# Batches of 768 tokens, 384 columns a matmul, in the last three products of an attention and two-MoE kernel

## The chip, the cores and the metric

The kernel runs on one core of one Trainium2 chip. The metric is the device time of one execution in microseconds. A core has a matrix engine (TensorE; PE in the profile, its weight loads PEld), a vector engine (DVE), a scalar engine (ACT), GpSimd (POOL) and SyncE (SP), which here issues all transfers, one after the other, from a single queue.

## What is computed

```python
# q, k, v: (8, 8, 576, 64), phi: (8, 8, 576, 32)
a = softmax(phi, axis=2)
k_m = einsum('bhsm,bhsd->bhmd', a, k)
v_m = einsum('bhsm,bhsd->bhmd', a, v)
attn = softmax(q @ k_m.T / 8) @ v_m
x = attn as 4608 tokens x 512
x = relu(x @ moe_w_in) ** 2 @ moe_w_out
h = x @ moe2_w_in
out = (h * sigmoid(h)) @ moe2_w_out        # 512 -> 2048 -> 512, twice
```

All is float32, and the weights come as float64 words, which the kernel itself turns into float32.

## The kernel before

Every product works on float32 numbers that are split into a high and a low part, and takes three matmuls for one (high by high, high by low, low by high). Four stages follow each other.

- **Stage 0** is the attention and the first MoE product (`front`, `first_product`, matmuls at L464), for eight batches of 576 tokens. Its result goes to DRAM in quarters, `g1`, one DMA for two of the sixteen rows of features (L476).
- **Stage 1** is the second MoE product, by `second` (matmuls at L641). **Stage 2** is the third product, by the loop at L718 (matmuls at L731). **Stage 3** is the fourth, by `second` again. These are the last three products of the title.

Stages 1 to 3 use Winograd's form of Strassen's scheme: a product of two-by-two blocks in seven block products instead of eight. `PRODUCTS` (L522) gives their seven right-hand sides in order, n = 0 to 6: B11, B21, T2, T1, T3, B22, T4. The T are differences of quarters of the tokens' matrix, and the seven left-hand sides are combinations of the weights, which `combine` makes on ACT and DVE in the stage before, writes to DRAM (L179) and `load_w` (L519) brings back. A tile `W[q]` holds all seven combinations for 256 rows or columns of the weights, q = 0 to 7; all eight tiles stay in SBUF for a stage. A combination with its high and low part is 256 KB.

A stage takes the tokens in eight batches of 576, as two halves of 288 columns. In `second` a batch is 7 products of 4 steps (h) of 12 matmuls, 336 in all, and the first and last product are 28 steps apart. Three steps ahead (`AHEAD`), `combos` makes the operand of a step: ACT casts the high part (L612), DVE subtracts it for the low part (L613); for n = 2 DVE makes four differences before (L602 T1, L604 T3, L608 T2, L609 T4). The quarters of a batch lie in six places that rotate from batch to batch (`places`, `NAMES`, `FREED`). In stage 2 a batch is four rounds r of two q, and a round is 7 products of 12 matmuls. `evict` adds and copies the sums out of PSUM.

A scheduler decides each engine's order; the instructions of an engine and the transfers of SP's queue then run strictly in that order, and a transfer that waits holds back those behind it. `hold` ties the background work of `combine` to a step of the product.

Of the kernel before, what the change touches and what calls it, by code (L numbers as in the profile page):

```python
# [18 lines left out]
P = 128  # L19
# [11 lines left out]
W4 = 512  # L31

# [3 lines left out]
GT = 3  # L36
# [29 lines left out]
def attention_moe_moe(ctx: ExitStack, tc, q, kv, phi, w_in1, w_out1, w_in2, w_out2, out):  # L66
# [53 lines left out]
    NQ = NF // 2  # L120
# [32 lines left out]
    def combine(key, srcs, following=None, whole=None, parts=None, step=None):  # L153
# [15 lines left out]
        def split(to, of):  # L169

            if whole is not None:
                hi, lo = whole[:, to, 0], whole[:, to, 1]
            else:
                part = prep.tile([P, 2, 2 * P], F32, tag="pp", bufs=2, name="pp")
                hi, lo = part[:, 0].bitcast(F32R), part[:, 1]
            held(nc.scalar.copy(hi, w[:, of]))  # L176
            tt(lo, w[:, of], hi.bitcast(F32), op=ALU.subtract)  # L177
            if whole is None:
                nc.sync.dma_start(parts[:, to], part)  # L179
# [48 lines left out]
    def load_unit(j, i):  # L228

        n = 2 * j + i  # L230
        if n < 3 * (NQ // 2):
            if n % 3 == 0:
                staged["w"] = wr.tile([P, 7, 4 * P], F32, tag=f"w{n // 3}", name="st")
            st = staged["w"].rearrange("p i c -> p (i c)")[:, n % 3 * 4 * PC:(n % 3 + 1) * 4 * PC]
        else:
            if i == 0:
                staged[j] = work.tile([P, 2, 2, W4], F32, tag="ring", bufs=RING, name="st")
# [13 lines left out]
    def front(b):  # L251
# [23 lines left out]
        def load_q(r):  # L275
            if b == 0 and r == 2:
                t = work.tile([P, 2, 2, HALF], F32, tag="gt", bufs=GT, name="q")
                t = t.rearrange("p a b n -> p (a b n)")[:, :NP * RT].rearrange("p (k n) -> p k n", k=NP)
# [170 lines left out]
    def quarters_tiles(n):  # L449
        return [dram.tile([P, NQ, 4, HALF], F32, tag=f"{n}_{b}", name=f"{n}_{b}") for b in range(B)]  # L450

# [3 lines left out]
    def first_product(t):  # L455
# [14 lines left out]
        if f % 2 == 0:  # L470
            gts[b] = work.tile([P, 2, 2, HALF], F32, tag="gt", bufs=GT, name="gt")
        gt = gts[b]
        nc.scalar.activation(gt[:, f % 2], h[:, :, :HALF], AF.Relu)  # L473
# [12 lines left out]
    for t in sorted(sched):  # L486
# [4 lines left out]
    W.update({q: wr.tile(WSHAPE, F32R, tag=f"w{q}", name=f"ws{q}") for q in range(NQ // 2)})  # L491
    background = combine_all([
        (("w1o", q), src_out(w_out1, q), {"whole": W[q]} if q in W else {"parts": w1o[q]}) for q in reversed(range(NQ))
# [22 lines left out]
    W.update({q: wl.tile(WSHAPE, F32R, tag=f"w{q}", name=f"ws{q}") for q in range(NQ // 2, NQ)})  # L516

    def load_w(src, q, n0, n1):
        nc.sync.dma_start(W[q][:, n0:n1].bitcast(F32), src[q][:, n0:n1])  # L519
# [3 lines left out]
    FIRST = (0, 1, 3)  # L523

# [27 lines left out]
    NAMES = ("B11", "B21", "B12", "B22", "T2", "")  # L552
    FREED = ("", "T2", "B11", "B12", "B22", "B21")

    def second(src, order, first_places, square, to, begin):
# [5 lines left out]
        places = [dict(zip(first_places, range(6)))]  # L561
        for _ in range(1, B):
# [3 lines left out]
        def place_tiles(b, name):  # L566

            i = places[b][name]
            if i < 2:
                t = xpool.tile([P, NQ, HALF], F32, tag="xt"[i], name="r")  # L570
                ts = [t[:, :HQ], t[:, HQ:]]
            else:
                ts = [xpool.tile([P, HQ, HALF], F32, tag="xc", bufs=8, name="r") for _ in range(2)]
# [5 lines left out]
        def quarters(b, names=("B11", "B21", "B12", "B22")):  # L579
            for name in names:  # L580
                for i, t in enumerate(place_tiles(b, name)):
                    for h in range(i * HQ, i * HQ + HQ, QS):
                        dma = nc.sync.dma_start(t[:, h - i * HQ:h - i * HQ + QS], src[b][:, h:h + QS, order.index(name)])
# [7 lines left out]
        def combos(b, n, h):  # L591
# [19 lines left out]
            c = cc[b, n, h] = spool.tile([P, 2, QS, HALF], F32R, tag="g", bufs=5, name="c")  # L611
# [3 lines left out]
        steps = [(b, n, h) for b in range(B) for n in range(7) for h in range(NH)]  # L615
# [12 lines left out]
        for k, (b, n, h) in enumerate(steps):  # L628
# [5 lines left out]
            if h == 0 and n in FIRST:  # L634
                for o in range(2):
                    ps[o][bank] = psum.tile([P, HALF], F32, tag=bank, bufs=4 if bank == "a" else 2, name=f"ps{bank}")
            x = cc.pop((b, n, h))
            for u in range(QS):
                for o in range(2):
                    for m, (wi, xi) in enumerate(((0, 0), (0, 1), (1, 0))):  # L640
                        mm = nc.tensor.matmul(  # L641
                            ps[o][bank], W[h * QS + u][:, n, wi, o * P:(o + 1) * P], x[:, xi, u],
# [3 lines left out]
                        if u == o == m == 0:  # L646
                            begun.append(mm)
            if h < NH - 1:
                continue
            for o in range(2):  # L650
                def tile_s(u, o=o):
                    if u not in st[o]:
                        st[o][u] = spool.tile([P, HALF], F32, tag=u, name=u)
                    return st[o][u]

                def done(c, bank, o=o, b=b):
                    if bank is None:
# [6 lines left out]
                evict(n, ps[o], tile_s, lambda c: tile_s(SUM[c]), nc.scalar.copy, done)  # L664

# [3 lines left out]
    x2 = [dram.tile([P, 2, NP, HALF], F32, tag=f"x2_{b}", name=f"x2_{b}") for b in range(B)]  # L669

    def begin_out1(quarters):
        quarters(0, ("B11",))
        for n, name in enumerate(("B21", "B12", "B22", None)):
            for q in range(NQ // 2, NQ):
                load_w(w1o, q, n, n + 1 if name else 7)
            if name:
                quarters(0, (name,))

    second(g1, ("B11", "B12", "B21", "B22"), ("B21", "", "B11", "B12", "B22", "T2"), True,
           lambda b, o, half: x2[b][:, half, o], begin_out1)  # L680
# [10 lines left out]
    xc = {}  # L691

    def load_x2(b):
        x = xpool.tile([P, 2, NP, HALF], F32, tag="x", name="x2")
        for half in range(2):
            nc.sync.dma_start(x[:, half], x2[b][:, half])
        tt = nc.vector.tensor_tensor
        t = xpool.tile([P, 4, 2, HALF], F32, tag="t", name="t2")
        tt(t[:, 0:2].rearrange("p h k n -> p h (k n)"), x[:, 1].rearrange("p (h k) n -> p h (k n)", h=2),
           x[:, :, 0:2].rearrange("p h k n -> p h (k n)"), op=ALU.subtract)  # L700
        tt(t[:, 2], x[:, 1, 2:4], t[:, 0], op=ALU.subtract)
        tt(t[:, 3], x[:, 0, 2:4], t[:, 2], op=ALU.subtract)
        xt[b] = {"B11": x[:, 0, 0:2], "B21": x[:, 0, 2:4], "B22": x[:, 1, 2:4],
                 "T1": t[:, 0], "T3": t[:, 1], "T2": t[:, 2], "T4": t[:, 3]}

    def split_x2(b, n):
        src = xt[b][PRODUCTS[n][0]]
        c = xc[b, n] = xpool.tile([P, 2, 2, HALF], F32R, tag="xc", bufs=8, name="xc")
        nc.scalar.copy(c[:, 0], src)
        nc.vector.tensor_tensor(c[:, 1], src, c[:, 0].bitcast(F32), op=ALU.subtract)  # L710

    load_x2(0)
    for n in range(7):
        for q in range(NQ):
            load_w(w2i, q, n, n + 1)
    for n in range(7):
        split_x2(0, n)
    for b in range(B):  # L718
        for r in range(NQ // 2):
# [3 lines left out]
            gq = {q: spool.tile([P, 4, HALF], F32, tag="g", bufs=5, name="g2t") for q in qs}  # L723
            for n, (_, bank) in enumerate(PRODUCTS):
                for q in qs:
                    if n in FIRST:
                        ps[q][bank] = psum.tile([P, HALF], F32, tag=bank, bufs=4 if bank == "a" else 2, name=f"ps{bank}")
                    x = xc[b, n]
                    for k in range(2):
                        for m, (wi, xi) in enumerate(((0, 0), (0, 1), (1, 0))):  # L730
                            mm = nc.tensor.matmul(  # L731
                                ps[q][bank], W[q][:, n, wi, k * P:(k + 1) * P], x[:, xi, k],
# [16 lines left out]
                if r == NQ // 2 - 1 and b + 1 < B:  # L749
                    split_x2(b + 1, n)  # L750
            for q in qs:
                nc.sync.dma_start(g2[b][:, q], gq[q])
            if r == 0 and b + 1 < B:
# [9 lines left out]
    def begin_out2(quarters):  # L763
        quarters(0, ("B11", "B21"))
        for q0, n0, n1 in ((0, 0, 4), (2, 0, 4), (4, 0, 2), (6, 0, 1), (6, 1, 2), (4, 2, 4), (6, 2, 3)):
            for n in range(n0, n1):
                for q in (q0, q0 + 1):
                    load_w(w2o, q, n, n + 1)
            if q0 == 6 and n0 == 1:
                quarters(0, ("B12", "B22"))  # L770
        for n in range(3, 7):
            for q in (range(NQ) if n > 3 else (6, 7)):
                load_w(w2o, q, n, n + 1)
# [48 lines left out]
```

## Time and profile before

| | us |
|---|---|
| median of 3 runs | 1471.46 (1466.14 to 1471.5) |
| the profiled execution, its time | 1474.32 |
| its span, first to last instruction | 1472.5 |
| TensorE busy | 1408.9 (96%) |
| DVE busy | 1070.2 (73%) |
| ACT busy | 825.8 (56%) |
| DMA | 321.40 MB, 218 GB/s over the span |

The time of an execution is the span and some 2 us around it. Busy times of TensorE count a matmul from its start to a modelled end, so consecutive ones overlap; its pace is read from the distance of starts.

### The profile page before, as it was taken

To read this page: it belongs to the slowest core of one execution; us is meant where nothing else is said; L and a number is where in the kernel's file an instruction comes from. 1 tells how busy PE (TensorE), PEld (TensorE's weight loads), DVE (VectorE), ACT (ScalarE), POOL (GpSimd) and SP (SyncE) were. 2 spreads that over 40 slices of the span, in tenths; PEclk is the share of its full clock that TensorE was granted. 3 is DMA by queue.
4 is the path that set the end of the run, shared out by engine and by line. 5 is a ranking of instruction groups with operands and counts; after the bars stand their busy time and mean duration, and the time that the engine had idled before them with its cause. 6 is when DMAs were issued, how large, how long until landed. Compare 5 with 4: busy or idle time off the path is not lost.

```text
span 1472.5 us, 29779 instructions
## 1 busy us (share of the span) xinstructions
PE 1408.9 (96%) x11264; PEld 1332.2 (90%) x11264; DVE 1070.2 (73%) x2078; ACT 825.8 (56%) x1582; POOL 44.6 (3%) x85
## 2 busy tenths in 40 slices
PE   4799999999999999999989999999998999999999
PEld 2567777778999999999989999999998999999999
DVE  5768787772798888998957666677536776677874
ACT  3455565566677777677545555555534444444443
POOL 2220100000000000000000000000000000000000
PEclk9899999999999999999999999999999999999999
DMA  9568988757955765458985564565599435354320
GB/s 358 164 220 306 322 318 303 242 190 269 358 176 196 238 211 193 159 196 268 328 288 200 207 229 181 208 225 220 211 397 320 121 102 157 121 153 138 112 90 33
DMA packets 184271, 321.40 MB, mean 218 GB/s; under 512 B 16192, under 2 KB 100672, under 8 KB 183616
## 3 DMA queue, kind: packets, MB, share of 16 engines
q1 hardware_dynamic: 184128, 319.50, 62.8%
q8 instruction: 88, 1.44, 0.4%
q14 instruction: 55, 0.45, 0.1%
HBM read 188.37 MB, written 131.07 MB: 217 GB/s over the span
## 4 chain that ended last, share of the span: by engine, by line
PE 66%; DVE 14%; DMA 12%; ACT 4%; issue 3%; SPq 1%; POOL 1%; ACTq 0%; POOLq 0%; DVEq 0%
PE psa L641 19%; PE psa L731 13%; PE psc L641 10%; PE h L464 7%; PE psc L731 6%; PE psb L641 4%; DVE c L613 4%; PE psb L731 3%; DMA kv<-kv 2%; DMA r<-g 2%; PE pswp L360 1%; ACT c L612 1%; DVE r L608 1%; DMA a<-phi 1%; DMA st<-moe_w_out 1%
## 5 line engine op out<-in xcount | busy, mean ns | idle before, releaser
L613 DVE TENSOR_TENSOR c<-r,c 128x576 fp32r<-128x576 f32 x448 | 332.0, 753 | 154.0 <-ACT c L612 151.3
L641 PE MATMUL psa<-c,ws 128*128 128x288 f32 x3072 | 429.3, 297 | 9.8 <-DVE c L613 6.0
L612 ACT CAST c<-r 128x576 fp32r<-128x576 f32 x448 | 298.0, 673 | 235.9 <-PE psa L641 119.9
L641 PEld LDWEIGHTS psa<-c,ws 128*128 128x128 f32 x3072 | 416.9, 190 | 13.4 <-DVE c L613 8.5
L464 PEld LDWEIGHTS h<-at,wp 128*128 128x128 f32 x1536 | 213.9, 194 | 56.7 <-ACT gt L473 26.3
L464 PE MATMUL h<-at,wp 128*128 128x288 f32 x1536 | 237.3, 308 | 14.6 <-ACT gt L473 10.4
L731 PE MATMUL psa<-xc,ws 128*128 128x288 f32 x1536 | 230.9, 296 | 4.7 <-ACT u L530 3.8
L731 PEld LDWEIGHTS psa<-xc,ws 128*128 128x128 f32 x1536 | 213.4, 188 | 5.3 <-ACT u L530 4.0
L641 PE MATMUL psc<-c,ws 128*128 128x288 f32 x1536 | 211.0, 295 | 0.0
L641 PEld LDWEIGHTS psc<-c,ws 128*128 128x128 f32 x1536 | 206.4, 188 | 0.0
L731 PE MATMUL psc<-xc,ws 128*128 128x288 f32 x768 | 118.1, 295 | 0.0
L473 ACT ACTIVATE gt<-h 128x576 f32<-128x576 f32 x128 | 82.1, 648 | 55.9 <-PE h L464 51.2
L641 PE MATMUL psb<-c,ws 128*128 128x288 f32 x768 | 109.4, 296 | 0.7 <-DVE c L613 0.7
L731 PEld LDWEIGHTS psc<-xc,ws 128*128 128x128 f32 x768 | 107.6, 188 | 0.0
L641 PEld LDWEIGHTS psb<-c,ws 128*128 128x128 f32 x768 | 104.4, 188 | 1.4 <-DVE c L613 1.4
L589 ACT ACTIVATE r<-r 128x576 f32<-128x576 f32 x128 | 85.1, 683 | 20.5 <-DMA r<-g 17.9
L176 ACT CAST pp<-pw 128x256 fp32r<-128x256 f32 x140 | 55.4, 404 | 51.0 <-DMA w1o<-pp 11.6
L177 DVE TENSOR_TENSOR pp<-pw,pp 128x256 f32<-128x256 f32 x140 | 57.4, 418 | 28.1 <-ACT pp L176 26.9
L745 ACT ACTIVATE g2t<-g2t 128x864 f32<-128x864 f32 x64 | 58.3, 923 | 31.1 <-DVE g2t L528 31.0
L530 ACT COPY u<-psa 128x288 f32<-128x288 f32 x96 | 37.5, 396 | 58.6 <-PE psa L731 40.3
L731 PE MATMUL psb<-xc,ws 128*128 128x288 f32 x384 | 63.5, 299 | 0.0
L535 ACT COPY u<-psa 128x288 f32<-128x288 f32 x96 | 37.8, 398 | 39.9 <-PE psa L731 33.4
(86 smaller groups left out, 1266.0 us busy)
## 6 DMA issues: line engine op xcount, KB each, us to landing
r<-g SPq DMA_DIRECT2D x256, 288.0 KB, 4.4
g<-gt SPq DMA_DIRECT2D x64, 576.0 KB, 4.7
g<-g2t SPq DMA_DIRECT2D x64, 576.0 KB, 4.0
kv<-kv SPq DMA_DIRECT2D x32, 516.0 KB, 6.6
st<-moe_w_out SPq DMA_DIRECT2D x64, 256.0 KB, 3.7
w2i<-pp SPq DMA_DIRECT2D x56, 256.0 KB, 3.2
ws<-w2i SPq DMA_DIRECT2D x56, 256.0 KB, 4.3
w2o<-pp SPq DMA_DIRECT2D x56, 256.0 KB, 2.7
```

The lines of the kernel that those rows point to most:

```text
L176: held(nc.scalar.copy(hi, w[:, of]))
L177: tt(lo, w[:, of], hi.bitcast(F32), op=ALU.subtract)
L464: mm = nc.tensor.matmul(h[:, half, :HALF], wp[b, j][:, g, s, fo:fo + P], attnT[b][:, x, g, tk], start=(k == 0), stop=(k == len(ops) - 1),)
L473: nc.scalar.activation(gt[:, f % 2], h[:, :, :HALF], AF.Relu)
L530: nc.scalar.copy(s("u1"), t["a"])
L535: nc.scalar.copy(s("u2"), t["a"])
L589: nc.scalar.activation(raw[b, name, h], raw[b, name, h], AF.Square)
L612: nc.scalar.copy(c[:, 0], r(name))
L613: tt(c[:, 1], r(name), c[:, 0].bitcast(F32), op=ALU.subtract)
L641: mm = nc.tensor.matmul(ps[o][bank], W[h * QS + u][:, n, wi, o * P:(o + 1) * P], x[:, xi, u], start=(n in FIRST and h == u == m == 0), sto ...
L731: mm = nc.tensor.matmul(ps[q][bank], W[q][:, n, wi, k * P:(k + 1) * P], x[:, xi, k], start=(n in FIRST and k == 0 and m == 0), stop=(k == ...
L745: nc.scalar.activation(gq[q][:, :3], gq[q][:, :3], AF.Silu)
```

## The change

- Stages 1 to 3 take six batches of 768 tokens (`TB`, `TH`): a half is 384 columns, so a matmul has 384 in place of 288, and there are three quarters as many of all instructions of a batch.
- `W[q]` holds six combinations in place of seven (`SLOTS`). Those for n = 1 and n = 6 share a place (`slot`): after product 1, `next_w` loads combination 6 over it, after product 6 combination 1 again, in every batch.
- Of the first four `W[q]`, which stage 0 fills directly, combinations 1 and 6 now go through DRAM too (`keep`).
- `second` has five places for quarters in place of six. T3 is written in the code at n = 3 and T4 at n = 4, no more at n = 2.
- Stage 0 still makes batches of 576. Its quarters go to DRAM in batches of 768, so each store is cut in two (of 384 and 192 columns). `g1` and `g2` keep a quarter's rows together.
- Sums `u1` and `u3` share buffers, `gt` has four in place of three, and the background work is held to other steps (`BEGIN2`, `PARTS`).

```diff
+TB, TH = 6, 384
-GT = 3
+GT = 4
+WR = 4
+SLOTS = 6
-STEPS = B * 7 * 4
-BEGIN2, SPREAD2 = 9, 28
-BEGIN3, SPREAD3 = 4, 24
-PARTS = (0, 1, 3, 4, 6, 8, 10, 12, 13, 15, 17, 19, 21)
+STEPS = TB * 7 * 4
+BEGIN2, SPREAD2 = 2, 20
+BEGIN3, SPREAD3 = 2, 18
+PARTS = (0, 1, 2, 3, 5, 6, 8, 9, 10, 12, 13, 15, 16)
...
-            if whole is not None:
+            keep = whole is not None and to not in (1, 6)
+            if keep:
...
-            nc.sync.dma_start(g1[b][:, u:u + 2, 2 * fh:2 * fh + 2], gt)
+            i = 0
+            while i < S:
+                to, k = divmod(b * S + i, TH)
+                n = min(TH - k, S - i)
+                nc.sync.dma_start(g1[to // 2][:, 2 * fh + to % 2, u:u + 2, k:k + n], gt[:, :, i:i + n])
+                i += n
...
+    def slot(n):
+        return n if n < SLOTS else 1
+
+    def load_w(src, q, n):
+        nc.sync.dma_start(W[q][:, slot(n)].bitcast(F32), src[q][:, n])
+
+    def next_w(src, qs, n, last):
+
+        if n == 1 or n == 6 and not last:
+            for q in qs:
+                load_w(src, q, 7 - n)
...
+    UTAG = {"u1": "u1", "u2": "u2", "u3": "u1"}
...
-    NAMES = ("B11", "B21", "B12", "B22", "T2", "")
-    FREED = ("", "T2", "B11", "B12", "B22", "B21")
+    NAMES = ("B11", "B21", "B12", "B22", "T2")
+    FREED = ("B11", "T2", "B12", "B22", "B21")
...
                 tt(r("B11"), r("B12"), r("B11"), op=ALU.subtract)
                 raw[b, "T1", h] = r("B11")
-                tt(r("B12"), r("B22"), r("B12"), op=ALU.subtract)
-                raw[b, "T3", h] = r("B12")
                 if h == 0:
                     place_tiles(b, "T2")
                 tt(r("T2"), r("B22"), r("T1"), op=ALU.subtract)
+            elif name == "T1":
+                tt(r("B12"), r("B22"), r("B12"), op=ALU.subtract)
+                raw[b, "T3", h] = r("B12")
+            elif name == "T3":
                 tt(r("B21"), r("B21"), r("T2"), op=ALU.subtract)
                 raw[b, "T4", h] = r("B21")
...
+            next_w(weights, range(h * QS, h * QS + QS), n, b == TB - 1)
...
+                next_w(w2i, qs, n, b == TB - 1)
```

Where the scheduler puts these things is seen at three places. The first is DVE at the start of stage 3, from the last but one operand of product 1 on. Before:

```order
L613 TENSOR_TENSOR c<-r,c 128x576 x3
L602 TENSOR_TENSOR r<-r 128x576
L604 TENSOR_TENSOR r<-r 128x576
L608 TENSOR_TENSOR r<-r 128x576
L604 TENSOR_TENSOR r<-r 128x576
L608 TENSOR_TENSOR r<-r 128x576
L609 TENSOR_TENSOR r<-r 128x576
L604 TENSOR_TENSOR r<-r 128x576
L608 TENSOR_TENSOR r<-r 128x576
L528 TENSOR_TENSOR u_13662<-psb,u_13662 128x288
L528 TENSOR_TENSOR u_13664<-psb,u_13664 128x288
```

Now (L620 is T1, L624 T2, L626 T3, L629 T4, L633 the low part):

```order
L620 TENSOR_TENSOR r<-r 128x768 x2
L633 TENSOR_TENSOR c<-r,c 128x768
L624 TENSOR_TENSOR r<-r 128x768
L626 TENSOR_TENSOR r<-r 128x768
L624 TENSOR_TENSOR r<-r 128x768
L626 TENSOR_TENSOR r<-r 128x768
L629 TENSOR_TENSOR r<-r 128x768
L633 TENSOR_TENSOR c<-r,c 128x768
L629 TENSOR_TENSOR r<-r 128x768
L624 TENSOR_TENSOR r<-r 128x768
L626 TENSOR_TENSOR r<-r 128x768
```

T3 and T4 still stand among the T2, ahead of product 3's operands; between the last operand of product 1 and the first of product 2 there are five differences now, where there were eight differences and two sums of `evict`.

The second place is SP's queue in the middle of stage 3, within one batch: `r<-g` loads quarters of the next batch, `out` stores results. Before:

```order
L663 DMA out<-u_14159 128x288
L663 DMA out<-u_14161 128x288
L583 DMA r<-g_2_9051 128x2x288 x9
L663 DMA out<-u_14373 128x288
L663 DMA out<-u_14375 128x288
L663 DMA out<-u_14307 128x288
L663 DMA out<-u_14309 128x288
L663 DMA out<-y 128x288 x2
```

Now (`ws` are places of the weights, loaded from `w2o`; L531 is `load_w`), from the quarters to the last result of the batch; eight more loads of the same kind, of combination 6, follow in the next batch:

```order
L602 DMA r<-g_1_8210 128x768 x11
L684 DMA out<-u_12143 128x384
L684 DMA out<-u_12145 128x384
L602 DMA r<-g_1_8210 128x768
L684 DMA out<-u_12073 128x384
L684 DMA out<-u_12075 128x384
L531 DMA ws_388<-w2o_11315 128x512
L531 DMA ws_389<-w2o_11316 128x512
L531 DMA ws_390<-w2o_11317 128x512
L531 DMA ws_391<-w2o_11318 128x512
L531 DMA ws_4535<-w2o_11319 128x512
L531 DMA ws_4536<-w2o_11320 128x512
```

Loads of weights, of which there were none inside a batch, now stand between the results of two products, in the order in which the products end.

The third place is SP's queue in the middle of stage 2, a little over one round: `g` are results, `st` and `w2o` belong to the background work. Before:

```order
L179 DMA w2o_13053<-pp 128x512 x3
L752 DMA g_4_9053<-g2t 128x1152 x2
L179 DMA w2o_13053<-pp 128x512
L752 DMA g_4_9053<-g2t 128x1152 x2
L129 DMA st<-moe_w_out 128x512
L179 DMA w2o_13054<-pp 128x512
```

Now:

```order
L531 DMA ws_4535<-w2i_7749 128x512
L531 DMA ws_4536<-w2i_7750 128x512
L183 DMA w2o_11320<-pp 128x512 x2
L132 DMA st<-moe_w_out 128x512 x2
L531 DMA ws_4535<-w2i_7749 128x512
L183 DMA w2o_11320<-pp 128x512
L531 DMA ws_4536<-w2i_7750 128x512
L779 DMA g_3_8212<-g2t 512x1x384
L531 DMA ws_4537<-w2i_7751 128x512
L779 DMA g_3_8212<-g2t 512x1x384
```

Each tile of weights is loaded twice a round (combination 6, then 1), and stores of the background work, which wait for DVE, stand between the two.

## Rows read from the trace of the kernel before

**Rows 1.** The page: engines' busy us, share of the span, instructions.
```profile
PE 1408.9 (96%) x11264; PEld 1332.2 (90%) x11264; DVE 1070.2 (73%) x2078; ACT 825.8 (56%) x1582; POOL 44.6 (3%) x85
```
**Rows 2.** Windows by stage: us, PE PEld DVE ACT POOL, clock, DMA, GB/s.
```profile
0.00:372.00 372.00, 325.60 (x3200) 253.92 (x3200) 253.03 (x574) 207.44 (x407) 44.58 (x85) 0.98 0.77 268
372.00:735.00 363.00, 360.36 (x2682) 358.19 (x2683) 324.60 (x591) 257.01 (x489) 0.00 (x0) 1.00 0.69 232
735.00:1101.00 366.00, 361.33 (x2698) 360.56 (x2697) 226.69 (x515) 187.95 (x398) 0.00 (x0) 1.00 0.64 236
1101.00:1472.50 371.50, 361.58 (x2688) 359.54 (x2686) 265.90 (x400) 173.43 (x290) 0.00 (x0) 0.99 0.43 137
```
**Rows 3.** The chain that ended last, in time: start us, us, what.
```profile
793.07 3.21 PE psa L731 x24
...
1150.36 12.75 PE psa L641 x96
1163.11 3.45 PE psb L641 x26
...
1207.74 3.45 PE psb L641 x26
```
**Rows 4.** Stage 3 near 1122 us: PE's timeline, forms, windows (as rows 2).
```profile
1122.78 5.00 PE L641 MATMUL psa<-c,ws 128*128 128x288 f32 x20
...
L641 PE MATMUL psa<-c,ws 128*128 128x288 f32 x20 | 5.0, 442 | 0.0
...
1121.10:1127.90 6.80, 5.53 (x23) 5.53 (x24) 6.57 (x11) 1.28 (x2) 0.00 (x0) 0.50 0.89 307
```
**Rows 5.** Timeline of PE around two short groups in stage 0: start us, us.
```profile
130.00 0.59 PE L310 MATMUL psmx<-dm,ones 128*128 128x256 f32 x2
130.22 0.38 PE L310 MATMUL psmx<-dm,ones 128*128 128x256 f32 x1
...
142.23 0.43 PE L464 MATMUL h<-at,wp 128*128 128x288 f32 x2
142.49 0.27 PE L347 MATMUL pst<-ident,y 128*128 128x128 f32 x1
```
**Rows 6.** Groups by form: matmuls and weight loads (busy us, mean ns of one).
```profile
L641 PE MATMUL psa<-c,ws 128*128 128x288 f32 x3072 | 429.3, 297 | 9.8 <-DVE c L613 6.0 <-ACT c L612 3.6
L641 PEld LDWEIGHTS psa<-c,ws 128*128 128x128 f32 x3072 | 416.9, 190 | 13.4 <-DVE c L613 8.5 <-ACT c L612 4.5 <-DMA ws<-w1o 0.2
L347 PEld LDWEIGHTS pst<-ident,y 128*128 128x128 f32 x32 | 4.2, 148 | 2.2 <-ACT y L338 1.6 <-issue 0.4 <-DVE wp L403 0.2
```
**Rows 7.** Groups by form: operations of DVE by length.
```profile
L613 DVE TENSOR_TENSOR c<-r,c 128x576 fp32r<-128x576 f32 x448 | 332.0, 753 | 154.0 <-ACT c L612 151.3
...
L699 DVE TENSOR_TENSOR t<-x 128x1152 f32<-128x1152 f32 x8 | 10.8, 1356 | 2.4 <-DMA x<-x 2.4
```
**Rows 8.** DMA issues: count, KB each, median us from issue to landing.
```profile
g<-gt SPq DMA_DIRECT2D x64, 576.0 KB, 4.7
...
ws<-w2i SPq DMA_DIRECT2D x56, 256.0 KB, 4.3
...
ws<-w2o SPq DMA_DIRECT2D x56, 256.0 KB, 6.0
```
**Rows 9.** Timeline of PE at the start of stage 3.
```profile
1118.68 0.42 PE L641 MATMUL psa<-c,ws 128*128 128x288 f32 x2
1122.37 8.87 PE L641 MATMUL psa<-c,ws 128*128 128x288 f32 x46 [3.27 <-DVE c L613]
```
**Rows 10.** Stage 2: SP's waits (us in total, times, longest), then SP's timeline.
```profile
SPq L179 <- DVE pp L177: 97.5, 40, 8.1
...
1089.80 9.62 SPq L519 DMA_DIRECT2D ws<-w2o  x13
```
**Rows 11.** Stage 2's start: timeline of PE.
```profile
742.27 1.81 PE L731 MATMUL psc<-xc,ws 128*128 128x288 f32 x12
747.90 2.47 PE L731 MATMUL psa<-xc,ws 128*128 128x288 f32 x12 [3.82 <-ACT u L530]
```

More of the change, by code (lines that the diff above doesn't have):

```diff
@@ L449, in quarters_tiles @@
     def quarters_tiles(n):
-        return [dram.tile([P, NQ, 4, HALF], F32, tag=f"{n}_{b}", name=f"{n}_{b}") for b in range(B)]
+        return [dram.tile([P, 4, NQ, TH], F32, tag=f"{n}_{b}", name=f"{n}_{b}") for b in range(TB)]
     g1 = quarters_tiles("g1")
@@ L490, in attention_moe_moe @@
             fn()
[L491 removed]
+    W.update({q: wr.tile([P, SLOTS, 2, 2 * P], F32R, tag=f"w{q}", name=f"ws{q}") for q in range(WR)})
     background = combine_all([
[L493 removed]
+        (("w1o", q), src_out(w_out1, q), {"whole": W.get(q), "parts": w1o[q]}) for q in reversed(range(NQ))
     ])
@@ L550, in attention_moe_moe, with x_tile, second @@
     AHEAD = 3
-    NAMES = ("B11", "B21", "B12", "B22", "T2", "")
-    FREED = ("", "T2", "B11", "B12", "B22", "B21")
-    def second(src, order, first_places, square, to, begin):
+    NAMES = ("B11", "B21", "B12", "B22", "T2")
+    FREED = ("B11", "T2", "B12", "B22", "B21")
+    def x_tile(i, shape, dtype, name):
+        return xpool.tile(shape, dtype, tag=f"x{i}", name=name)
+    def second(src, order, square, to, weights, begin, tiles=tuple(range(10))):
         raw = {}
         cc = {}
-        places = [dict(zip(first_places, range(6)))]
-        for _ in range(1, B):
+        places = [dict(zip(NAMES, range(5)))]
+        for _ in range(1, TB):
             was = places[-1]
@@ L568, in place_tiles @@
             i = places[b][name]
[L569 to L573, printed above, removed]
+            ts = [x_tile(tiles[2 * i + k], [P, HQ, TH], F32, "r") for k in range(2)]
             for h in range(NH):
@@ L664, in second @@
                 evict(n, ps[o], tile_s, lambda c: tile_s(SUM[c]), nc.scalar.copy, done)
+        return [tiles[2 * places[-1][name] + k] for name in FREED for k in range(2)]
     SUM = {"C11": "u1", "C22": "u3", "C12": "u2"}
-    x2 = [dram.tile([P, 2, NP, HALF], F32, tag=f"x2_{b}", name=f"x2_{b}") for b in range(B)]
+    x2 = [dram.tile([P, 2, NP, TH], F32, tag=f"x2_{b}", name=f"x2_{b}") for b in range(TB)]
     def begin_out1(quarters):
         quarters(0, ("B11",))
[L673 to L680, printed above, removed]
+        for n, name in enumerate(("B21", "B12", "B22")):
+            for q in range(0 if n == 1 else WR, NQ):
+                load_w(w1o, q, n)
+            quarters(0, (name,))
+        for n in range(3, SLOTS):
+            for q in range(WR, NQ):
+                load_w(w1o, q, n)
+    free = second(g1, ("B11", "B12", "B21", "B22"), True, lambda b, o, half: x2[b][:, half, o], w1o, begin_out1)
     w2i = scratch("w2i")
@@ L767, in begin_out2 @@
                 for q in (q0, q0 + 1):
-                    load_w(w2o, q, n, n + 1)
+                    load_w(w2o, q, n)
             if q0 == 6 and n0 == 1:
                 quarters(0, ("B12", "B22"))
-        for n in range(3, 7):
+        for n in range(3, SLOTS):
             for q in (range(NQ) if n > 3 else (6, 7)):
-                load_w(w2o, q, n, n + 1)
-    second(g2, tuple(c.replace("C", "B") for c in order2), NAMES, False,
-           lambda b, o, half: out[b, :, o, half * HALF:(half + 1) * HALF], begin_out2)
+                load_w(w2o, q, n)
+    second(g2, tuple(c.replace("C", "B") for c in order2), False,
+           lambda b, o, half: out[b, :, o, half * TH:(half + 1) * TH], w2o, begin_out2, free)
 _INS = ["q", "k", "v", "phi", "moe_w_in", "moe_w_out", "moe2_w_in", "moe2_w_out"]
```

81 lines of the change are left out of this document (41 added, 40 removed).

## The prediction

> **What bounds the kernel now.** I read the page first. TensorE is busy for 96% of the span, DVE for 73%, ACT for 56% [rows 1]; an edit counts if it shortens TensorE's stream or makes TensorE wait. The windows by stage [rows 2] part the 1472.5 us: 372 for stage 0, which keeps its form but for the stores of `g1`, and 363, 366 and 371.5 for stages 1, 2 and 3, 1100.5 together, in which the change works.
>
> How much of that is the bare stream of matmuls? The chain of what ended last goes through PE, and in it 96 matmuls of L641 take 12.75 us: 132.8 ns each [rows 3]. The two rows of L641 psb there, 1163.11 and 1207.74, stand one batch of 336 matmuls apart, 44.63 us, again 132.8 ns; stage 2's 24 matmuls of L731 in 3.21 us give 133. A stage of eight batches is 8 x 44.63 = 357.0 us, three are 1071; the other 29 are starts, ends and waits. So the time of a matmul of 384 columns decides, and the trace has none.
>
> What it shows of 288: at 2.4 GHz, with granted clock 1.00 [rows 2], 288 columns are 120.0 ns, so a matmul takes 12.8 ns more than its columns. Near 1122 us the granted clock is 0.50, the level of 1.2 GHz; 20 matmuls take 5.00 us there from the first start to the last end; less the 0.442 that one takes from start to end, 4.56 over 19, or 240 ns [rows 4]: 288 / 1.2 exactly. With the stream at half speed the 12.8 ns are hidden. They aren't cycles of TensorE that each matmul adds, then, but something that runs beside the stream and is the slower of the two at 2.4 GHz: fixed for a matmul, growing with its columns, or partly both.
>
> **The change part by part.** *Matmuls.* There are 6 x 336 = 2016 a stage in place of 2688, and columns as before in all. The bounds of the new duration: below, the excess is a fixed floor that a longer stream covers, 384 / 2.4 = 160 ns. Above, it is a rate of 132.8 / 288 = 0.461 ns a column: 177.1 ns, and 2016 x 177.1 = 357 us, no gain. The weight load could be such a floor, since one stands beside each matmul with 190 ns to the matmul's 297 [rows 6]. The short groups in stage 0 speak against it: behind a 288-column matmul that starts with its twin at 142.23, L347 with its shorter load (148 ns) starts at 142.49, again 0.13 us a matmul [rows 5, 6]. Against a bare rate stands one pair: the second matmul psmx starts 0.22 us after the first [rows 5], 256 columns in full float32, which is two passes and 213 ns at 2.4 GHz. A long stream pays little there, but two passes ask for half the columns in a ns, so this doesn't exclude the rate. I take the value between: the 12.8 ns stay once a matmul, 160 + 12.8 = 172.8. A batch takes 336 x 172.8 = 58.06 us, a stage 348.4: -8.7, in three stages **-26**. That is nearer to the upper bound (0) than to the lower (2016 x 160 = 322.6 a stage, -34.5 each, -103 in all before other costs).
>
> The Trainium skill, "TensorE: Matmul & The Clock Gate", section "Back-to-back issue gap", gives N/2.4 + 2.5 ns for a matmul at full clock, N/1.2 at half. The trace agrees at half clock (240) and not at full: it would be 122.5 ns, and 132.8 are measured. By it 384 columns are 162.5 ns, and the three stages' streams 6048 x 162.5 = 983 us, 88 less than now; no run here shows that.
>
> *Operands and sums.* DVE takes 753 ns for 576 elements and 1356 for 1152 [rows 7]: 603 for 576 more, 1.047 ns each, so 954 for 768. Low parts go from 448 x 753 = 337 us to 336 x 954 = 321 over stages 1 and 3. DVE, the fullest beside TensorE (324.6 us of stage 1's 363, 0.89 [rows 2]), falls to about 311 of 354, 0.88. It keeps its distance, and costs nothing while the stream takes 354 us; if a stage took 328, DVE would stand at 0.95 and be late at times. The moved T3 and T4 move little, as the order shows.
>
> *Weights loaded again.* `next_w` is run at n = 1 in six batches, at n = 6 in five, for eight q: 88 loads of 256 KB a stage, less the eight that are no longer loaded ahead, 80 x 0.262 MB = 21 MB. Stage 1 moves 232 GB/s x 363 us = 84 MB now [rows 2]; with 105 in 354 us it is 297 GB/s. A share of 0.69 carries 232 there, so 297 is 0.88, about the 0.89 (307 GB/s) of the window near 1122 [rows 4]. Stage 2: 86 to 107 MB, 301 GB/s, 0.82; stage 3: 51 to 72 MB, 0.62. Packets can be carried; lateness has to be looked at. In `second` the load of combination 6 is issued after product 1's last use of a q and needed four products later, some 84 matmuls or 14.5 us at 172.8; a load lands 4.3 to 6.0 us after its issue [rows 8]. Cover enough: nothing. In stage 2 both q of a round are used in every product; combination 6 of the first may be loaded when its six matmuls in product 1 are done, and is needed 6 + 48 = 54 matmuls later, 9.3 us. Landing 4.3 to 6.0 and an issue on SP of 9.62 / 13 = 0.74 us [rows 10, 8] make 5 to 6.7: 2.6 us of slack at worst. Ahead of it in SP's queue, as the order shows, can stand a store of the background work that waits for DVE: 40 such waits come to 97.5 us in stage 2, 2.4 each, the longest 8.1 [rows 10]. A mean wait passes, the longest takes some 5 us of TensorE, and what is queued behind (g2's stores, the next tokens) is late with it. Nothing to 24 rounds x 5; I take **+3**, for few waits are far above the mean.
>
> *Stage borders.* Stage 2 starts with TensorE idle for 3.82 us after its first 23 matmuls [rows 11]; the loads of product 1's weights for the first round must now wait for the shared place and come late in SP's queue, needed 12 matmuls (2 us) in. Nothing to 5; I take **+2**. Stage 3 starts with 3.27 us behind DVE's c, then runs at half clock for 6.8 us [rows 9, 4]; in the order five differences stand ahead of product 2's first operand instead of eight and two sums, longer by a third: 5 x 0.95 in place of 8 x 0.75 and the sums. **-1**, at most -3.
>
> *Stores of g1.* 64 of 576 KB, landing in 4.7 us [rows 8], become 128 of a third and two thirds that. 64 more issues of SP at 0.74 are 47 us of SP's time spread over 372 us, with DMA share 0.77 [rows 2]; TensorE waits only if a `gt` comes free late, and there are four of these now. Nothing to +6; **+2**.
>
> Sum: -26 - 1 + 3 + 2 + 2 = -20. The profiled execution took 1474.3, 2.9 above the median of 1471.5: 1454.3 by its own time, 1451.4 by the median's. I forecast **1453**, 1.3% faster.
>
> **The rivals.** *The excess has gone* (E). The psmx pair speaks for it, with under 2 ns beyond its columns. At 162 ns the streams are 1071 - 6048 x 0.162 = 91 shorter; DVE at 0.93 to 0.95 and the DMA at 0.9 in stages 1 and 2 take, by my estimate, some 20 of it back: 1474 - 91 + 6 + 20, by the median's level about 1405. Against it: no row shows a 288-column matmul below 130 ns, whatever its load. The Trainium skill's formula above comes to this case.
>
> *It is a rate* (C). Half clock with no excess at all speaks for it: something that delivers 2.17 columns a ns is hidden by 1.2 and not by 2.4. Then the stream is 357 a stage as before, and 3 + 2 + 2 - 1 = 6 less a little slack are left: 1475, no change. [...]
>
> *Stage 2's weights come late* (L), which ends slower. It decides once landing and hold pass 9.3 us: 6.0 + 0.74 + a hold of 2.6, just above the mean wait. If half of the 24 rounds lose 3 us, it is +36 in place of +3, 1486; if each loses 2, 1498. The order puts loads and waiting stores side by side, and two more loads a round move them closer. Against it: the waits are SP's idle time of before, and a store that waits ahead of the load may be done before it is due.
>
> *The change doesn't do what it says:* T3 and T4 aren't made later on DVE, as the order shows; that part is worth the -1 above and no time of its own. Five places in place of six could delay the quarters, but their loads have most of a batch, 58 us, for it.
>
> **How the numbers follow.** The forecast 0.50 (own range 1440 to 1464: the excess between 8 and 15 ns, the small terms at their bounds); E 0.14, C 0.18, L 0.18. To hold 8 in 10, the range goes from E's upper part to L's lower: 1408 to 1488. This kernel's measurement tells about 0.5%, 7 us, from no change. Faster: the forecast, E, and a little of L where the gain covers it, less where the forecast ends weak: 0.61. Same: C and that weak end, 0.19. Slower: L, and C with dearer borders, 0.20.
>
> **What would show it.** L661's distance of starts in a full stretch: 172 to 173 ns for the forecast, 160 to 163 for E, 177 for C. Windows of stages 1 and 3 about 355 and 360, 328 to 335 for E. PE's waits for DMA in stage 2: below 5 us in all; L shows them before product 6's matmuls with `ws<-w2i` as releaser. SP's waits for DVE ahead of L531 tell how near it came. The first product's stage stays within 372 to 375, or the stores of g1 cost more than I say. I'm wrong above all if a matmul isn't near 173 ns.

## The result and the profile after

The changed kernel took 1456.99 us (median of 5, 1452.04 to 1458.39), 0.990 of the kernel before (95% interval 0.987 to 0.993); 1453 was forecast. The profiled execution took 1452.04, its span 1450.3: 22.2 less than the span before, where the medians differ by 14.5. Profiled executions of kernels with the same stage 0 issue the last matmul of that stage between 366.3 and 373.7 us, so a few us of any single one are its own.

The page's engines, then the windows by stage (columns as in [rows 2]), of the kernel after:

```profile
PE 1386.1 (96%) x9248; PEld 1309.9 (90%) x9248; DVE 1045.2 (72%) x1800; ACT 790.7 (55%) x1328; POOL 44.9 (3%) x85
...
0.00:370.00 370.00, 321.86 (x3200) 250.61 (x3200) 254.62 (x574) 209.55 (x407) 44.89 (x85) 0.95 0.83 282
370.00:732.50 362.50, 357.21 (x2015) 354.76 (x2016) 318.23 (x489) 244.23 (x384) 0.00 (x0) 0.99 0.85 287
732.50:1087.50 355.00, 352.05 (x2014) 351.41 (x2014) 217.67 (x439) 175.17 (x321) 0.00 (x0) 1.00 0.86 302
1087.50:1450.30 362.80, 355.01 (x2023) 353.14 (x2021) 254.70 (x299) 161.79 (x218) 0.00 (x0) 0.99 0.60 200
```

TensorE is as full as before [rows 1] with 2016 fewer matmuls. The gain is uneven: stage 2's window is 11 us shorter, stage 3's nearly 9, stage 1's half a microsecond [rows 2]. The windows are cut by hand, a few matmuls off; counted by the starts of 2016 matmuls (2688 before), stage 2 is 9.2 us shorter, stage 3 10.1, stage 1 1.1. The chain that ended last, in stage 3, gives the pace that [rows 3] gave before:

```profile
1145.83 16.71 PE psa L661 x96
...
1187.64 8.35 PE psa L661 x48
1196.00 8.35 PE psc L661 x48
1204.35 16.71 PE psa L661 x96
```

16.71 / 96 is 174.1 ns, and the two long rows stand 58.52 us apart, one batch: 58.52 / 336 = 174.2. A stage's stream is 2016 x 174.15 = 351.1 us in place of 357.0. And stage 1's gain is eaten here, in the same view:

```profile
386.11 5.35 DMA st<-moe_w_in
391.46 0.02 issue
391.48 0.02 ACT pw L144
391.51 0.32 issue
391.82 0.82 ACT c L632
392.65 0.04 issue
392.69 1.01 PE psc L661 x2
```

ACT's cast of T1's first operand (L632) stands behind a conversion of background work (L144) that waits for words of `moe_w_in`, and TensorE waits for the cast. TensorE's order shows why it asks for the cast so early (a row is a run of matmuls on TensorE, `psb` product 1, `psc` product 3, the second `psa` product 2):

```
L661 MATMUL psb<-c,ws_4538 128x384 x6
L661 MATMUL psc<-c,ws_388 128x384 x2
L661 MATMUL psa<-c,ws_388 128x384 x4
L661 MATMUL psa<-c,ws_389 128x384 x6
```

Two matmuls of product 3 stand ahead of 46 of product 2, whose first operands are ready. Before the change 14 of product 2 stood ahead of those two. The matmuls behind the wait run at half clock (0.50) for some 5 us:

```profile
393.70:398.50 4.80, 4.80 (x17) 4.80 (x16) 3.63 (x7) 0.83 (x1) 0.00 (x0) 0.50 1.04 393
```

Worked out from the distances of starts, less 174.1 ns each, 6.1 us are lost between 389.5 and 398.8: 3.2 in the wait, the rest behind it. All of TensorE's waits in stages 1 to 3 (us in all, times, longest):

```profile
PE psa L661 <- DVE c L633: 4.3, 5, 2.6
PE psc L661 <- ACT c L632: 3.1, 1, 3.1
PE psa L757 <- ACT u L549: 2.6, 1, 2.6
PE psa L661 <- ACT c L632: 2.4, 2, 1.5
PE psb L661 <- DVE c L633: 1.1, 1, 1.1
PE psa L757 <- DVE g2t L547: 0.4, 1, 0.4
```

No row names a transfer: no matmul waited for weights. SP's waits of stage 2 show the reloads early rather than late:

```profile
SPq L531 <- PE psa L757: 58.9, 45, 6.7
SPq L183 <- DVE pp L181: 47.2, 23, 5.0
```

The loads (L531) stand at the queue's head and wait until TensorE has left the shared place; the stores that wait for DVE fell to 23 waits and 47 us, from 40 and 97.5 [rows 10].

### The profile page after: what moved, and what is told of

The parts are those of the page before. It is cut to its first block, busy times and chain, and to the rows that moved or that the text cites. A ratio compares the mean times of both kernels' runs of the same rounds, so it can differ in the third digit from the quotient of the medians.

```text
span 1450.3 us, 25489 instructions
## 1 busy us (share of the span) xinstructions
PE 1386.1 (96%) x9248; PEld 1309.9 (90%) x9248; DVE 1045.2 (72%) x1800; ACT 790.7 (55%) x1328; POOL 44.9 (3%) x85
## 4 chain that ended last, share of the span: by engine, by line
PE 76%; DMA 11%; DVE 8%; ACT 2%; issue 1%; SPq 1%; POOL 0%; ACTq 0%; POOLq 0%; DVEq 0%
PE psa L661 25%; PE psc L661 14%; PE psa L757 13%; PE psc L757 7%; PE h L468 6%; PE psb L661 5%; PE psb L757 3%; DMA w1o<-pp 2%; DMA st<-moe_w_out 2%; DMA kv<-kv 1%; DMA ws<-w1o 1%; PE pswp L364 1%; DMA st<-moe_w_in 1%; DMA r<-g 1%; DVE c L633 1%
## 5 line engine op out<-in xcount | busy, mean ns | idle before, releaser
L633 DVE TENSOR_TENSOR c<-r,c 128x768 fp32r<-128x768 f32 x336 | 318.5, 957 | 154.6 <-ACT c L632 153.4
L661 PE MATMUL psa<-c,ws 128*128 128x384 f32 x2304 | 419.0, 340 | 6.7 <-DVE c L633 4.3
L661 PEld LDWEIGHTS psa<-c,ws 128*128 128x128 f32 x2304 | 407.0, 190 | 9.7 <-DVE c L633 6.5
L632 ACT CAST c<-r 128x768 fp32r<-128x768 f32 x336 | 278.8, 834 | 237.9 <-PE psa L661 128.3
L757 PE MATMUL psa<-xc,ws 128*128 128x384 f32 x1152 | 221.1, 338 | 2.9 <-ACT u L549 2.6
L661 PE MATMUL psc<-c,ws 128*128 128x384 f32 x1152 | 207.0, 337 | 3.1 <-ACT c L632 3.1
L757 PEld LDWEIGHTS psa<-xc,ws 128*128 128x128 f32 x1152 | 203.6, 189 | 3.6 <-ACT u L549 2.9
L661 PEld LDWEIGHTS psc<-c,ws 128*128 128x128 f32 x1152 | 201.1, 188 | 3.6 <-ACT c L632 3.6
L757 PE MATMUL psc<-xc,ws 128*128 128x384 f32 x576 | 111.1, 336 | 0.0
L661 PE MATMUL psb<-c,ws 128*128 128x384 f32 x576 | 105.1, 337 | 1.2 <-DVE c L633 1.1
L661 PEld LDWEIGHTS psb<-c,ws 128*128 128x128 f32 x576 | 100.6, 188 | 1.9 <-DVE c L633 1.8
L757 PEld LDWEIGHTS psc<-xc,ws 128*128 128x128 f32 x576 | 100.9, 188 | 0.0
L608 ACT ACTIVATE r<-r 128x768 f32<-128x768 f32 x96 | 80.2, 844 | 17.3 <-DMA r<-g 16.4
L771 ACT ACTIVATE g2t<-g2t 128x1152 f32<-128x1152 f32 x48 | 54.8, 1162 | 28.5 <-DVE g2t L547 26.3
L144 ACT ACTIVATE pw<-st 128x256 f32<-128x256 f32 x96 | 40.7, 434 | 39.3 <-DMA st<-moe_w_out 16.9
L364 PE MATMUL pswp<-win,kvm 64*32 64x512 f32 (+1 forms) x576 | 47.8, 583 | 10.6 <-DVE ssm L382 3.8
```

Of the source, the lines that this page charges most:

```text
L144: ins = nc.scalar.mul(f.bitcast(F32), w1.bitcast(F32), 2.0 ** -112)
L364: nc.tensor.matmul(ps[m, g], st["kvm"][d, s, m], x(p)[d], start=True, stop=True)
L608: nc.scalar.activation(raw[b, name, h], raw[b, name, h], AF.Square)
L632: nc.scalar.copy(c[:, 0], r(name))
L633: tt(c[:, 1], r(name), c[:, 0].bitcast(F32), op=ALU.subtract)
L661: mm = nc.tensor.matmul(ps[o][bank], W[h * QS + u][:, slot(n), wi, o * P:(o + 1) * P], x[:, xi, u], start=(n in FIRST and h == u == m == 0 ...
```

## The experiments

The theory under test: each matmul pays some 13 ns beside its columns, longer matmuls pay it less often, and what else the change moved comes out at the starts of the stages. The rivals were a rate a column, contention in the full kernel, and a cost of the reloads all along. Ratios are to the kernel before, run on the same chip as the experiment.

**The matmul by itself.** Streams of 96 matmuls, with one width after the other:

```diff
+    def stream(n, count, w, x, step=1):
+        for m in range(count):
+            nc.tensor.matmul(
+                banks[m // 12 % 8][:, :n], w[:, m * step % 8], x[:, m % 3, :n],
+                start=(m % 12 == 0), stop=(m % 12 == 11), skip_group_check=True,
+            )
```

> This kernel leaves the whole computation out: after a warm-up it runs streams of 96 float32r matmuls each, of 512, 448, 384, 320, 288, 256, 192, 144 and 128 columns, nothing else beside them, then 288 and 384 again, both with one weight tile loaded anew each time, and both in bfloat16 and in full float32. Theory (a fixed price a matmul): the distance of starts is columns / 2.4 + 13 ns, so 226 ns at 512, 173 at 384, 133 at 288, 93 at 192, 66 at 128. Rival 1 (a rate, 0.454 to 0.461 ns a column): 232 to 236 at 512, 174 to 177 at 384, 131 to 133 at 288, 87 to 89 at 192, 58 to 59 at 128. Rival 2 (the price is contention with DVE, ACT and the transfers of the full kernel): without them 160 to 163 at 384 and 120 to 123 at 288.

The groups by form (count, busy us, mean ns of one); `raw` is full float32, `x` float32r, `xb` bfloat16:

```profile
L39 PE MATMUL b<-raw 128*128 128x384 f32 x192 | 62.1, 486 | 0.0
...
L39 PE MATMUL b<-raw 128*128 128x288 f32 x192 | 46.7, 406 | 0.0
...
L39 PE MATMUL b<-x,w 128*128 128x448 f32 x96 | 19.6, 365 | 0.0
L39 PE MATMUL b<-xb,wb 128*128 128x384 bf16 x96 | 15.8, 326 | 0.0
L39 PE MATMUL b<-x,w 128*128 128x320 f32 x96 | 14.2, 309 | 0.0
L39 PE MATMUL b<-xb,wb 128*128 128x288 bf16 x96 | 11.9, 286 | 0.0
L39 PE MATMUL b<-x,w 128*128 128x256 f32 x96 | 11.7, 283 | 0.0
L39 PE MATMUL b<-x,w 128*128 128x128 f32 x96 | 10.9, 274 | 0.0
L39 PE MATMUL b<-x,w 128*128 128x192 f32 x96 | 10.9, 274 | 0.0
L39 PE MATMUL b<-x,w 128*128 128x144 f32 x96 | 10.9, 275 | 0.0
```

Busy time less one matmul's length, over the distances, is the pace: (14.2 - 0.31) / 95 = 146 ns at 320, 120 at 256, 202.5 at 448. From the starts themselves: 226.7 at 512, 173.3 to 173.6 at 384, 131.7 to 132.2 at 288. So it is columns / 2.4 and 12 to 16 ns, 13.3 at most widths, with nothing running beside it: from 256 columns up the fixed price is right, rate (232 or more at 512) and contention (163 at most at 384) are wrong. 288 columns pay the least, 12, and 448 the most, 16; no run shows why. Below, the theory missed: 128, 144 and 192 columns all take 112 ns, a floor, where 66 and 93 had been expected at 128 and 192. One weight tile loaded again and again changes nothing (173.3 and 131.7). In bfloat16 the same widths take (15.8 - 0.33) / 95 = 162.9 and 122.3. A float32 matmul is recorded as two, each of twice its columns: 322.6 and 242.4. Both forms pay 2 to 3 ns; the 13 belong to float32r.

**Halves of 192 columns.**

```diff
-                        mm = nc.tensor.matmul(
-                            ps[o][bank], W[h * QS + u][:, slot(n), wi, o * P:(o + 1) * P], x[:, xi, u],
+                        for i in range(2):
+                            half = slice(i * TH // 2, (i + 1) * TH // 2)
+                            mm = nc.tensor.matmul(
+                                ps[o][bank][:, half], W[h * QS + u][:, slot(n), wi, o * P:(o + 1) * P], x[:, xi, u, half],
```

> The changed kernel, with each matmul of L661 (the second and the fourth product) as two of 192 columns. Fixed price of 13 ns: the pair takes 2 x (80 + 13) = 186 in place of 174, stages 1 and 3 grow by 2016 x 12 = 24 us each, +47 us in all. Rate: the pair takes 174 to 177, 0 to +6 us a stage. If a weight load is the limit for short matmuls (it may not fit beside 80 ns of columns), the pair takes far more than 186 and each stage over 60 us more.

1637.74 us in one run, 181 more than the changed kernel. A window of 300 us inside stage 1:

```profile
400.00:700.00 300.00, 298.36 (x2660) 297.33 (x2660) 209.06 (x324) 167.31 (x268) 0.00 (x0) 1.00 0.63 210
```

300 / 2660 is 112.8 ns a matmul, the floor measured alone. The third expectation held: the pair takes 226, not 186. The rate is refuted again, but for narrow matmuls a fixed price isn't the rule either: by these numbers the floor takes over where 13.3 + columns / 2.4 comes under 112, by estimate at some 235 columns; 192 and 256 were run, nothing between.

**No reloads.** `next_w` loads nothing.

```diff
-        if n == 1 or n == 6 and not last:
+        if False:
```

> The changed kernel without the reloads of the shared place: product 6 is computed with combination 1 of the weights, and some 21 MB a stage aren't read. Theory (reloads are hidden): stages 2 and 3 as before them, within 2 us each, DMA share of stage 2 about 0.65 in place of 0.86; at most the stall near 392 us in stage 1 shrinks, where the background's load of words landed late, 0 to -6 us in all. Rival (reloads delay other transfers and weights all along): -10 us or more, spread over the three stages.

1449.5 us, 0.984 (0.982 to 0.986). By the times that is 6 to 7 us below the changed kernel (1455.29 and 1456.99 in two runs), by the ratios 7 to 9: between the theory's span (0 to 6) and the rival's (10 or more). The loss in stage 1 stayed (5.1 us near 395), so the reloads don't cause it; in the one profiled execution stage 3's start lost 2.2 us in place of 7.0 and stage 2's start 7.2 in place of 4.8.

**The background work later.**

```diff
-BEGIN2, SPREAD2 = 2, 20
+BEGIN2, SPREAD2 = 9, 20
```

> The changed kernel with the background work of stage 1 held to step 9 in place of step 2 (BEGIN2 as before the change), nothing else. Theory: the 6.1 us lost between 392.7 and 398.8 (a wait of 3.1 us for ACT's cast, which stood behind a conversion that waited for words, and the half clock after it) come from the background's early start: stage 1 shortens by 4 to 6 us, the kernel by 0.3 to 0.4%. Rival: the wait is the first weights and quarters of the stage that crowd the queue; then the cast is late by as much for another reason, and the time is the same within 1 us.

1452.93 us, 0.987 (0.985 to 0.989). The loss near 392.7 fell from 6.1 to 1.3 us, as expected. Stage 2's start lost 6.9 us; the changed kernel lost 4.8 there in one profiled execution and 6.3 in the other, so that the later background work costs anything there isn't shown. In the time the gain is 2 to 4 us, and the intervals overlap.

**The changed kernel again**, as the measure for the next three:

> The changed kernel itself once more, as the measure for the runs beside it on the same chip. Expected 0.985 to 0.993 of the kernel before.

1455.29 us, 0.989 (0.987 to 0.991). Its profiled execution shows how far one repeats the other: near 393 it lost 4.8 us (6.1 in the first), at stage 2's start 6.3 (4.8), near 1110 4.4 (4.3).

**T3 and T4 early again.**

```diff
+                tt(r("B12"), r("B22"), r("B12"), op=ALU.subtract)
+                raw[b, "T3", h] = r("B12")
                 tt(r("T2"), r("B22"), r("T1"), op=ALU.subtract)
-            elif name == "T1":
-                tt(r("B12"), r("B22"), r("B12"), op=ALU.subtract)
-                raw[b, "T3", h] = r("B12")
-            elif name == "T3":
                 tt(r("B21"), r("B21"), r("T2"), op=ALU.subtract)
```

> The changed kernel with T3 and T4 written at n = 2 again, as before the change, everything else as changed. The prediction gave this part at most 1 us, since the scheduler puts T3 and T4 among the T2 either way: the same as the changed kernel within 0.2%. Rival (the later T3 and T4 carry part of the gain, through the starts of stages 1 and 3): stage 3's stall near 1109 us, 2.9 us and the half clock behind it, grows by 3 us or more, and stage 1's start likewise, so 0.3% slower or more.

1452.3 us, 0.987 (0.985 to 0.990): no slower, as the theory had it. The profile shows why that is no plain zero. At stage 3's start 7.1 us are lost in place of 4.3, so T3 and T4 are worth 2.8 there; but near 393 only 1.3 are, since the two matmuls of product 3 now stand behind 14 of product 2.

**Reloads on GpSimd's queue.**

```diff
-                load_w(src, q, 7 - n)
+                load_w(src, q, 7 - n, nc.gpsimd)
```

> The changed kernel with the reloads of the shared place (next_w alone) issued by GpSimd in place of SyncE, whose queue has nothing else in stages 1 to 3. Theory (the reloads cost next to nothing where they are): the time of the changed kernel within 0.2%, with SP's waits for PE ahead of L531 gone, some 80 us in stage 2. Rival (reloads that wait for TensorE hold back stores and quarters in SP's queue, and TensorE pays for it): 4 us or more faster. If GpSimd's way of issuing is slow, product 6 of stage 2 waits for its weights and the kernel is slower.

1467.65 us, 0.997 (0.996 to 0.998), 12 us slower than the changed kernel: neither theory. The reloads land as fast as before (3.5 to 5.5 us) and no product waits for them. The chain shows what TensorE does wait for, at the same place as before:

```profile
391.30 10.78 DMA st<-moe_w_in
...
402.10 0.02 ACT pw L144
...
402.43 0.83 ACT c L632
...
403.31 1.01 PE psc L661 x2
```

The words for the background work take 10.78 us in place of 5.35, and 11.1 us are lost there, 6.2 more than in the run of the changed kernel beside it. The transfers issued between 380 and 396 us show what runs beside them:

```profile
ws<-w1o POOLq DMA_DIRECT2D x8, 256.0 KB, 5.8
st<-moe_w_in SPq DMA_DIRECT2D x2, 256.0 KB, 10.4
```

In the changed kernel all eight reloads follow the words in SP's queue (words at 386.11, first reload at 387.46). Here GpSimd issues them from 386.73 to 394.40, before and behind the words (391.30). The transfers move no more for that: 389 GB/s while the words are under way, 387 in the changed kernel. That the reloads took their share from the words fits these rows; no run tests it by itself. The profiled executions differ by 12.7 us: stage 1 by 7.7, stage 0, with the same instructions, by 3.7, stage 3 by 1.7; for the part outside stage 1 no cause is shown.

**Three waits taken away.**

```diff
-BEGIN2, SPREAD2 = 2, 20
+BEGIN2, SPREAD2 = 6, 19
...
-                tt(r("B12"), r("B22"), r("B12"), op=ALU.subtract)
+                t3 = tt(r("B12"), r("B22"), r("B12"), op=ALU.subtract)
+                if b == 0:
+                    hold(t3)
...
+                if b == 0:
+                    hold(t4)
...
-            if r == 0 and b + 1 < TB:
+            if r == 1 and b + 1 < TB:
                 load_x2(b + 1)
```

> The changed kernel with three waits taken away: the background work of stage 1 begins at step 6 and is spread over 19 steps a tile in place of 2 and 20; T3 and T4 of a stage's first batch are tied to TensorE's step, so that they come after T2's operands; the next tokens of stage 2 are loaded in its second round in place of its first, so that DVE doesn't wait for them ahead of the background work. Theory (stalls and the half clock behind them at the stage starts are what is left between the stream and the time): stage 1 -5, stage 2 -3 to -5, stage 3 -3, in all 8 to 13 us below the changed kernel. Rival (the stalls move to the next late thing): less than 4 us.

1447.32 us, 0.983 (0.981 to 0.985): 8 below the changed kernel. Stage 1's loss is gone and stage 3's went from 4.4 to 1.5; stage 2's start still lost 5.1, between the 4.8 and 6.3 of the changed kernel, so that mend shows no effect. Its chain names the buffer:

```profile
735.77 6.52 DMA x<-y
742.28 0.02 issue
742.30 0.04 ACTq L549
742.34 0.04 issue
742.38 0.49 ACT u L549
742.87 0.04 issue
742.91 3.73 PE psa L761 x12
```

**And y in another buffer.**

```diff
-                        y = spool.tile([P, TH], F32, tag="u1", name="y")
+                        y = spool.tile([P, TH], F32, tag="u2", name="y")
```

> The version with three waits taken away, and the last result y of a batch in a buffer of u2 in place of u1. There, stage 2 begins with 5.1 us lost near 742.9, where ACT's first copy u1 waits for the store of stage 1's last y out of the same buffer. Theory (that buffer is the cause): the loss near 743 shrinks to 2 us or less and the kernel is 2 to 5 us below the version before this edit (0.983 of the kernel before). Rival (the conversions of the background work ahead of the copy on ACT, which wait for stores in the same queue, hold it as long): the loss stays above 3.5 us and the time is the same within 1.5 us.

1444.23 us, 0.980 (0.978 to 0.982), 3 below the version before it, with intervals that overlap; the profile is clearer: the loss moved to 749 and shrank to 1.2 us. In the changed kernel too the chain runs through this store (`x<-y`, 6.23 us from 737.02) to that copy. The rows of TensorE's waits, with L661 now L665 and L757 now L761:

```profile
PE psa L665 <- DVE c L637: 4.3, 9, 0.8
PE psa L665 <- ACT c L636: 2.4, 2, 1.5
PE psb L665 <- DVE c L637: 1.4, 2, 1.1
PE psa L761 <- ACT u L549: 1.0, 1, 1.0
```

No wait is longer than 1.5 us. This is the fastest version that computes the whole.

**T3 and T4 tied to TensorE's step, alone.** The `hold` lines of the version with three waits taken away, on the changed kernel.

> The changed kernel with T3 and T4 of a stage's first batch tied to TensorE's step, nothing else, so that two differences stand ahead of T2's first operand at the start of stage 3 in place of five. Theory: the 4.4 us lost near 1110 (a wait of some 2.9 us for DVE and the half clock behind it) shrink to 1.5 us, 2 to 3 us in all, 0.2%. Rival: the quarters' transfers arrive as late as DVE, and less than 1 us is won.

1447.92 us, 0.982 (0.979 to 0.985), 7 to 9 below the changed kernel. More than expected: stage 3's start lost 1.5 us in place of 4.3, as the theory said, and the loss near 393 vanished too, with the background work as early as in the changed kernel. ACT waits for the words even longer (4.8 us in place of 3.0), but the scheduler has put all of product 2 ahead of product 3's two matmuls. So it takes both: words that land late with the cast behind them (the later background takes that away), and two matmuls that ask for the cast too early (this edit and T3 early take that away). Within the intervals this one edit gives the time of the version with three waits taken away.

**The mended version without reloads.** Product 6 uses combination 1; the edit is that of the first run without reloads.

> The version with y in a buffer of u2, without the reloads of the shared place: product 6 is computed with combination 1 of the weights. It asks what the reloads cost once the stalls at the stage starts are mended. Theory (the 6 us that the kernel without reloads was below the changed one lie at the starts of stages 1 and 3): 0 to 3 us below the version with reloads. Rival (a cost in every batch): 5 us or more below.

1438.75 us, 0.977 (0.975 to 0.979), 5.5 below the version with reloads, so the rival by the time. The profiles don't bear out its cost in every batch: stages 1 to 3 as one window each, with reloads, then without:

```profile
371.30:1435.50 1064.20, 1056.55 (x6048) 1051.90 (x6048) 788.14 (x1226) 580.31 (x921) 0.00 (x0) 1.00 0.79 266
```

```profile
368.20:1431.90 1063.70, 1057.58 (x6048) 1053.39 (x6048) 790.38 (x1226) 581.36 (x921) 0.00 (x0) 1.00 0.59 201
```

The two differ by 0.5 us there, and by 3.1 in stage 0, where both run the same instructions. But the 0.5 is a sum of differences that cancel. By 2016 starts each, without reloads stage 3 took 351.2 us in place of 355.3, stage 2 350.5 in place of 351.9, stage 1 362.2 in place of 357.1. Stage 3 was shorter in the first pair too, 353.3 in place of 358.2. With reloads the loss lies at its start: 4.2 us between 1081 and 1104, with these waits, and the rest of the stage runs at the stream's pace:

```profile
PE psa L665 <- DVE c L637: 1.7, 4, 0.8
PE psa L665 <- ACT c L636: 0.9, 1, 0.9
```

Without them no wait is left from 1078 to 1125. So a cost of 4 to 5 us at one border stands in both pairs, and none in every batch. What brings it isn't shown: SP's queue and TensorE's order there differ both. Why stage 1 was 5.1 us longer in this one execution stays open.

## Why the prediction held

- **The matmul: the mechanism right, the size off.** "The 12.8 ns stay once a matmul, 172.8" measured 174.1 to 174.2, since the excess is 14.1 ns. The term "-26" is 3 x (351.1 - 357.0) = -18. The argument that weight loads aren't the limit held too: matmuls with a weight load each go down to 112 ns, under the 133 of the kernel before. The argument from half clock, that the excess runs beside the stream, pointed equally to the rate, and only the stream by itself decided that. The Trainium skill, "TensorE: Matmul & The Clock Gate", section "Back-to-back issue gap", gives N/2.4 + 2.5 ns for an isolated matmul: bfloat16 with 162.9 and 122.3 agrees, float32r with 173.4 and 132 doesn't. The rival that the excess has gone (1405) fell with it, as 174 were measured.
- **DVE and the transfers: right in the shares.** An operation of 768 elements took 957 ns (954 said), DVE's share of stage 1 is 318 / 362.5 = 0.88 (0.88 said, as 311 / 354: the stage is longer), the DMA shares are 0.85, 0.86 and 0.60 (0.88, 0.82 and 0.62 said).
- **Weights late in stage 2, "+3": not borne out.** TensorE waited for none, and the holds behind DVE's stores became shorter. The rival of late weights is refuted: the loads stood at the head of SP's queue before TensorE had left the place. Leaving the reloads out gives some 6 us or more in the times (two pairs), of which 4 to 5 lie at stage 3's start, where the prediction put no cost of theirs. The cover of 84 matmuls that it gives for combination 6 in `second` is combination 1's, from product 6 to the next batch's product 1; combination 6 has 228.
- **Stage 2's start, "+2": the cause named wrongly.** 4.8 and 6.3 us were lost in the two executions, against 5.7 before. It isn't the weights of product 1 but ACT's first `u1`, which waited for the store of `y` out of the same buffer, as moving `y` showed.
- **Stage 3's start, "-1": right in sign, too small.** The loss near 1109 is 4.3 us against 6.0 before; T3 and T4 late are worth 2.8 there. In the whole kernel their effect can't be told from none. Another 2.5 were won at the stage's first operands (2.7 lost against 5.2), where the prediction didn't look.
- **Stage 0, "+2": not to be told.** The profiled stage was 2 us shorter, inside what stage 0 differs by from one execution to the next.
- **What no step had: stage 1's 6.1 us (4.8 in the second execution).** The prediction costed the shift of the background work (`BEGIN2`, `PARTS`) at nothing, without naming its cover: the products whose operands are ready. The orders of TensorE and ACT would have shown that two matmuls give it up. So stage 1's window is 362.5 us, not the 355 that the prediction named as a sign.

So -26 + 6 came out as -18 + 3.5 by the medians: a stream term 8 too large and other terms 2 to 3 too dear. Behind the second number stand larger misses. By the starts in the two profiled executions of the changed kernel, stage 1 lost 5 and 7 us more beyond its stream than before, stage 2 3 and 2 less, stage 3 4 less in both, stage 0 2 and 1 less. That the forecast came within 4 us of the median is in part luck.

## What to carry to other kernels

Price a longer matmul by the excess over columns at the granted clock, and measure it alone in the same number format: one stream over several widths decides between a fixed price, a rate and a floor, where a trace with a single width can't. After such a change look at the first 25 us of each stage: here three waits of 3 us, with the half clock behind them, were worth 0.8% together, nearly as much as the change itself. Those mends weren't tried on the kernel before, so how much of the 2% needs the 768 tokens stays open. Before moving transfers to a second queue, look whether the transfer engines are full: here the queue added nothing where they were.

## What the runs showed of the hardware

- A float32r matmul costs 12 to 16 ns beyond its columns at 2.4 GHz (13.3 at 256, 320 and 384), where bfloat16 and each recorded half of a float32 matmul cost 2 to 3. In the full kernel it is 14, so DVE, ACT and 290 GB/s of transfers add at most 1 ns.
- At 1.2 GHz it costs nothing that shows: 240 ns for 288 columns [rows 4], and by the starts from 393.2 on, behind the wait in stage 1, 320 for 384.
- A float32r matmul with its weight load takes 112 ns at least, whether it has 128, 144 or 192 columns. Which of the two sets this isn't shown.
- Near 391 us in stage 1, where the transfer engines are full (a share of 1.04 and 1.05), a second queue adds nothing: 389 GB/s with GpSimd's reloads beside SP's transfers, 387 with SP's alone; the reloads landed in 5.8 us, the words of SP's queue in 10.4 in place of 5.4.
